# Softmax readings summed by a GpSimd DMA, one query buffer, a power root, and a new plan

## The chip, the core and the metric

The kernel runs on one core of one Trainium2 chip. The metric is the device time in microseconds of one execution; lower is better. The core's engines run side by side and meet at semaphores: PE (matmul), ACT (activation functions), DVE (vector work), POOL (GpSimd) and SP, which here only issues DMAs. SBUF is the on-chip memory, PSUM the eight banks into which PE writes.

## What is computed

Multi-query attention and a feed-forward block, both fed by the same layer norm, added to the input. Sequence S = 2048, width D = 640, 32 heads of 20 with one shared K and V, feed-forward width 1728, all in bf16:

```python
xn = _layernorm(x)
q = (xn @ wq).reshape(B, S, 32, 20).transpose(0, 2, 1, 3)
k = xn @ wk
v = xn @ wv
scores = einsum("bhqd,bkd->bhqk", q, k) * 20 ** -0.5
o = einsum("bhqk,bkd->bhqd", softmax(scores), v)
return x + o.transpose(0, 2, 1, 3).reshape(B, S, 640) @ wo + silu(xn @ w1) @ w2
```

## The kernel before

**Blocks.** The scores are cut into 2048 blocks of 128 keys by 512 queries for one head: 4 query chunks (`QC`), 8 groups of four heads per chunk, 16 key tiles. A step (`do_S`, matmuls at L1133) multiplies three or four blocks at once, each in a strip of 32 rows of PE, one PSUM bank per block. The value product PV (`do_pv`, L973) takes up to four items at once, one per head of the group, each in a strip of 32 columns.

**Two ways to the exponential.** Most blocks go to ACT: one activation (L1167) over one to three banks writes the exponentials into a ring `E` of 31 blocks, and each block is one PV item. The others go to DVE. The scores come out of PE scaled so that, clipped and converted to int16 (L1182, called p1), their bits read as bf16 are a coarse exponential. To make it finer, it is read three times: as it is (`Z`), and with 43 and with 86 added to the bits (`Y`, two planes). Each reading is multiplied by its own copy of V, weighted 1.0, 0.8047 and 0.625, in PSUM. So a DVE block is three PV items. Three DVE blocks make a set; `flush_z` issues a set's two additions, on POOL as 64-bit integer additions over the set (L1221, after a load of the library that holds them, `go_wide`; before that as 32-bit ones, L1227), or the first of them on DVE (L1215). `NZ` = 4 sets of buffers rotate.

**The rest of PE's work.** `mm4` (L872) does the query projections, the feed-forward block and the output projection, in jobs that fill in between steps. Tanh on ACT (L1379) with L1384 on DVE makes the SiLU. When a group of four heads is done, DVE copies its PSUM bank out (L1285), an SP transpose turns it (L1254), and L1269 and L1275 normalise it.

**The planner.** The program builds its own order. `Sched` holds one list per engine and modelled durations for each operation; it walks through modelled time, and at each moment picks the next instruction of each engine. What it chose is fixed in the program: the engines run in that order and wait on semaphores. `SEG` is a table of 64 rows, each for 32 score blocks, with the planner's thresholds: how much DVE backlog still lets a block go to DVE (`DVE_TH`, `DVE_TH2`), when PV may run, and so on. Its rows have a value that no name in `SEG_KEYS` takes, the last. An operation marked `lock` isn't planned on POOL and DVE at the same time; `late` is added to the modelled landing of a DMA.

**Queries.** `qT` holds the queries of two chunks, in two buffers. `qd_job` projects 128 columns for a chunk and DMAs copy its heads into their strips; two big copies (`qz`) fill the strips' constant rows first.

**The prologue.** Sixteen tiles of x are loaded, their mean and variance are taken on DVE (L1685, L1687) or, for the tiles in `ACT_STATS`, on ACT (L1670, L1673). The reciprocal root runs in batches of tiles (`BATCHES`) as two Newton steps, chains of some ten small instructions on POOL (`newton`, L1734 to L1758). The norm is applied on DVE (L1715) or POOL (L1711), the result is transposed by SP or PE. K and V follow; a second copy of K with an offset is made on POOL (L1838), the weighted copies of V on DVE (L1860).

Of the kernel before, what the change touches and what calls it, by code (L numbers as in the profile page):

```python
# [8 lines left out]
BF16 = mybir.dt.bfloat16  # L9
# [26 lines left out]
UT_LATE = 2.0  # L36
# [12 lines left out]
OFF_LO = 45.0  # L49
PH = ((0, 1.0), (43, 0.8046875), (86, 0.625))  # L50
# [5 lines left out]
NZ = 4  # L56
# [5 lines left out]
H0_STEP = 10  # L62
# [25 lines left out]
FOUR_FROM = 35  # L88
# [7 lines left out]
PV_HOLD = 12  # L96
# [3 lines left out]
DT = (5, 6, 7, 8, 9, 10, 11, 12, 14, 15)  # L100
NORM_P = 0.9
# [14 lines left out]
K1_ENG = "pool"  # L116
PV_MIN = 3
PV_GO = 9
PRO = "t0 t2 t1 p0 t3 k0 k1 p1 q1 v0 t4 k2 v1 k3 k4 t13 v2 k5 k6 v3 k7 d0"
ACT_STATS = (1, 4, 6, 12, 14, 15)  # L120
NW_ENG = ("pool", "pool", "pool")
NORM_ENG = ("pool", "dve", "dve", "dve", "pool", "dve", "dve", "dve", "dve", "pool", "dve", "pool")
# [5 lines left out]
            "ACT4", "SPLIT", "U2", "LOOK", "JOB_BANKS", "U_IDLE")  # L128
SEG = (
# [64 lines left out]
)  # L194
BATCHES = ((0, 4), (4, 10), (10, 16))
T_ACT = (0, 2, 6)


# [288 lines left out]
class Builder:  # L487
# [205 lines left out]
    def s_reads(self, bs, dvs=()):  # L693
        k = []
        for x in bs:
            g, kt, j = x
            c, h = g // 8, 4 * (g % 8) + j
            k += [("kT1" if x in dvs else "kT", kt // 2), ("kT", kt // 2), ("qb", c % 2, h)] + self.qkeys(c, h)
# [1242 lines left out]
```

## Time and profile before

| | us |
|---|---|
| median of 3 runs | 662.92 (662.53 to 663.67) |
| the profiled execution | 662.48 |
| its span, first to last instruction | 660.7 |
| clock of TensorE granted | 1.000 |
| the exponentials on ACT (L1167), 644 activations | 609.6 |
| p1 on DVE (L1182), 739 blocks | 476.4 |
| integer additions on POOL (L1221), 491 | 394.1 |
| PV matmuls (L973), 3526 | 266.7 |

The profile gives, for each engine, the time in which an instruction of it was running. PE's busy time overlaps with itself, since matmuls are pipelined and their ends are modelled. A line such as L1182 is the line of the program which recorded the operation. "Idle before" is the time in which an engine stood still ahead of a group's instructions, and the releaser is what ended most of it.

### The profile page before, as it was taken

To read this page: it belongs to the slowest core of one execution; us is meant where nothing else is said; L and a number is where in the kernel's file an instruction comes from. 1 tells how busy PE (TensorE), PEld (TensorE's weight loads), DVE (VectorE), ACT (ScalarE), POOL (GpSimd) and SP (SyncE) were. 2 spreads that over 40 slices of the span, in tenths; PEclk is the share of its full clock that TensorE was granted. 3 is DMA by queue.
4 is the path that set the end of the run, shared out by engine and by line. 5 is a ranking of instruction groups with operands and counts; after the bars stand their busy time and mean duration, and the time that the engine had idled before them with its cause. 6 is when DMAs were issued, how large, how long until landed. Compare 5 with 4: busy or idle time off the path is not lost.

```text
span 660.7 us, 22924 instructions
## 1 busy us (share of the span) xinstructions
PE 654.3 (99%) x9762; PEld 220.6 (33%) x9764; DVE 601.5 (91%) x1060; ACT 645.8 (98%) x735; POOL 420.3 (64%) x568
## 2 busy tenths in 40 slices
PE   8999999999999999999999999999999999999998
PEld 4432222323333333333333333333332333333334
DVE  7799999899999997999999979999999998999995
ACT  7899999999999999999999999999999999999995
POOL 6646667676776662676666744677666664766673
PEclk9999999999999999999999999999999999999999
DMA  7566300000004200001003210000000310011001
GB/s 212 97 237 195 88 18 11 10 13 13 14 20 72 73 10 10 10 10 18 18 11 57 63 39 10 18 10 8 12 19 10 77 55 25 10 18 34 11 10 42
DMA packets 52058, 27.89 MB, mean 42 GB/s; under 512 B 37910, under 2 KB 51318, under 8 KB 51958
## 3 DMA queue, kind: packets, MB, share of 16 engines
q1 hardware_dynamic: 50502, 26.22, 15.6%
q8 instruction: 78, 1.28, 0.8%
q10 hardware_dynamic: 1456, 0.22, 0.2%
q14 instruction: 22, 0.18, 0.1%
HBM read 11.44 MB, written 2.62 MB: 21 GB/s over the span
## 4 chain that ended last, share of the span: by engine, by line
PE 92%; ACT 3%; DVE 2%; DMA 2%; SPq 1%; issue 0%; DVEq 0%
PE psall L973 34%; PE psall L1133 29%; PE psall L872 27%; ACT sbt L1167 3%; DMA sbt<-sbt 1%; DVE sbt L1685 1%; DMA sbt<-in_A_x_dram 1%; SPq L1575 0%; DVE sbt L1715 0%; PE psall L1828 0%; PE psall L1369 0%; PE psall L1851 0%; ACT sbt L1379 0%; DVE sbt L1467 0%; DVE sbt L1820 0%
## 5 line engine op out<-in xcount | busy, mean ns | idle before, releaser
L1167 ACT ACTIVATE sbt<-psall 128x1024 bf16<-128x1024 f32 (+2 forms) x644 | 609.6, 1068 | 3.5 <-PE psall L1133 2.9
L1221 POOL INT64_ADD sbt<-sbt x491 | 394.1, 815 | 209.1 <-DVE sbt L1182 183.8
L1182 DVE TENSOR_SCALAR sbt<-psall 128x512 int16<-128x512 f32 x739 | 476.4, 684 | 37.1 <-PE psall L1133 27.6
L973 PE MATMUL psall<-sbt 128*32 128x512 bf16 x3526 | 266.7, 383 | 0.0
L1133 PE MATMUL psall<-sbt 32*128 32x512 bf16 x2048 | 243.6, 384 | 0.3 <-ACT sbt L1167 0.2
L872 PE MATMUL psall<-sbt 128*32 128x320 bf16 (+2 forms) x3939 | 218.3, 331 | 0.3 <-DVE sbt L1687 0.3
L1133 PEld LDWEIGHTS psall<-sbt 32*128 32x128 bf16 x2048 | 61.8, 91 | 235.2 <-issue 80.8
L872 PEld LDWEIGHTS psall<-sbt 128*32 128x32 bf16 x3939 | 85.6, 95 | 85.1 <-issue 50.2
L973 PEld LDWEIGHTS psall<-sbt 128*32 128x32 bf16 x3526 | 63.3, 95 | 99.5 <-issue 68.9
L1384 DVE SCALAR_TENSOR_TENSOR sbt<-sbt,psall 128x512 bf16<-128x512 bf16 x54 | 36.7, 682 | 6.5 <-ACT sbt L1379 6.0
L1379 ACT ACTIVATE sbt<-psall 128x512 bf16<-128x512 f32 x54 | 33.6, 629 | 0.4 <-PE psall L872 0.3
L1285 DVE CAST sbt<-psall 128x512 bf16<-128x512 f32 x32 | 21.9, 683 | 0.6 <-PE psall L973 0.4
L1275 DVE TENSOR_TENSOR sbt<-sbt 128x320 bf16<-128x320 bf16 x31 | 15.8, 510 | 0.0
L1448 DVE SCALAR_TENSOR_TENSOR sbt<-psall,sbt 128x320 bf16<-128x320 f32 x28 | 13.5, 484 | 1.6 <-PE psall L872 1.2
L848 PE MATMUL psall<-sbt 128*128 128x512 bf16 (+2 forms) x44 | 12.9, 447 | 1.4 <-DVE sbt L1624 1.2
L1467 DVE SCALAR_TENSOR_TENSOR sbt<-psall,sbt 128x320 bf16<-128x320 f32 x28 | 13.0, 482 | 1.2 <-PE psall L872 1.2
L1336 DVE TENSOR_SCALAR sbt<-psall 128x512 bf16<-128x512 f32 (+1 forms) x19 | 12.9, 678 | 0.1
L1685 DVE BATCH_NORM_STATS2 sbt<-sbt 128x6 f32<-128x320 bf16 x20 | 8.9, 471 | 3.4 <-DMA sbt<-in_A_x_dram 3.4
L1269 DVE RECIPROCAL sbt<-sbt 128x16 f32<-128x16 bf16 x31 | 7.6, 244 | 0.4 <-DMA sbt<-sbt 0.4
L848 PEld LDWEIGHTS psall<-sbt 128*128 128x128 bf16 x46 | 4.8, 112 | 7.5 <-issue 3.3
L1227 POOL TENSOR_TENSOR sbt<-sbt 128x768 int32<-128x768 int32 x4 | 5.9, 1465 | 0.5 <-DVE sbt L1182 0.5
L1464 ACT ACTIVATE sbt<-psall 128x320 bf16<-128x320 f32 x4 | 1.6, 437 | 4.4 <-PE psall L872 4.3
(72 smaller groups left out, 90.8 us busy)
## 6 DMA issues: line engine op xcount, KB each, us to landing
sbt<-in_A_x_dram SPq DMA_DIRECT2D x32, 160.0 KB, 3.7
out_dram<-sbt SPq DMA_DIRECT2D x15, 160.0 KB, 2.0
sbt<-in_B_w_dram SPq DMA_DIRECT2D x5, 432.0 KB, 5.3
sbt<-sbt SPq DMA_DIRECT2D x105, 20.0 KB
sbt<-in_B_w_dram SPq DMA_DIRECT2D x13, 160.0 KB, 3.0
sbt<-sbt SPq DMA_DIRECT2D x1, 1024.0 KB, 6.3
sbt<-sbt SPq DMA_TRANSPOSE x57, 2.5
sbt<-in_A_wo_dram SPq DMA_DIRECT2D x5, 160.0 KB, 3.0
```

The source lines that it names most:

```text
L848: return pe.matmul(self.bk(b, 0, n), self.zero[:, 0:P], self.zero[:, 0:n], start=True, stop=True)
L872: ins = pe.matmul(self.bk(b, 0, n, r, r + SLOT), w[:, r:r + SLOT], x, start=start, stop=stop, tile_position=(0, r), skip_group_check=True)
L973: ins = pe.matmul(self.bk(ub[k], 0, QW, r, r + SLOT), self.v[:, it.w, it.kt, :], it.x(), start=f, stop=False, tile_position=(0, r), skip_g ...
L1133: ins = pe.matmul(self.bk(bank[x]), self.kT[r:r + SLOT, kk, kt * P:(kt + 1) * P], self.qT[r:r + SLOT, g % 8, (g // 8) % 2, :], start=True, ...
L1167: return a.activation(self.E[:, b0 * QW:(b0 + na) * QW].rearrange("p (b n) -> p b n", n=QW), src, AF.Exp, scale=ACT_SCALE)
L1182: return v.tensor_scalar(self.Z[:, zs, zp * QW:(zp + 1) * QW], self.bk(bb), 0.0, ZMAX, ALU.max, ALU.min)
L1221: sc.new("pool", tp, lambda v, k=k, c=c: v.int64_add(self.Y[:, zs, k, 0:w].bitcast(I64), self.Z[:, zs, 0:w].bitcast(I64), c), zk + [("lib" ...
L1275: op = sc.new(eng, 0.067 + 16 * DH / 960.0, lambda v: v.tensor_tensor(dst, ut[:, :, :, 0:DH], rb, ALU.mult), [key, ("rL", up)], [("o", h0 ...
L1285: sc.new("dve", t_dve_ps(QW), lambda v: v.tensor_copy(self.U[:, up, :], self.bk(ub)), [("B", ub)], [("U", up)], prio=U_PRIO, name=f"Uev{g}")
L1379: sc.new("act", t_act(QW), lambda a: a.activation(t, src, AF.Tanh, scale=0.5), [("B", b)], [("tb", tp)], prio=TH_PRIO, name=f"th{c}_{fk}") ...
L1384: sc.new("dve", t_dve_ps(QW), lambda v: v.scalar_tensor_tensor(out=self.hT[0:rows, fk, :], in0=t, scalar=1.0, in1=src, op0=ALU.add, op1=AL ...
L1685: np_("dve", 0.41, lambda v, hf=hf: v.bn_stats(self.st6[:, n, hf, :], x[:, hf * 320:hf * 320 + 320]), self.xkeys(n), [("st6", n, hf)], pri ...
```

## The change

**Summed readings.** The offsets are 0, 41 and 87 now, and the first two readings carry the same weight, so V is kept in two copies: one for the readings 0 and 41, one for 87. Where `both` holds in `flush_z`, a DMA issued by POOL adds the set's `Z` to its first `Y` plane (384 KB, bf16), and each block becomes two PV items; elsewhere it stays three. `both` needs a full set, the loaded library, and a modelled POOL backlog (with the two additions, 1.6 us) under the new threshold `CB_TH`, the last value of the `SEG` rows. Of the 64 rows, 39 have it above 1.6 and 26 above 4; the 39 are rows 4, 6, 8, 10, 12, 14, 15, 16, 18, 19, 20, 23, 24, 26, 28, 30, 32 to 40, 42, 44, 46, 48, 50 to 54, 56, 58 and 60 to 62, counted from 0; most of the others have -9. The DMA is booked with 1.2 us on POOL and a landing of some 3.4 us more.

**Buffers.** `qT` holds one chunk instead of two; the second constant fill goes. `NZ` becomes 5.

**Prologue.** The Newton chains become an addition and a power on POOL, in six batches instead of three. The norm on POOL adds the negative mean and then multiplies. The second copy of K is made on DVE, so the library of 64-bit additions is loaded as soon as POOL's prologue work is done. ACT's table load goes ahead of the loads of wk and wv. Five tiles instead of six have their statistics on ACT, six instead of four their norm on POOL.

**Order.** Every row of `SEG` is new, and so are the order of the first jobs (`PRO`), some modelled times and thresholds, and with them the whole order of instructions.

```diff
-UT_LATE = 2.0
+UT_LATE = 3.0
-PH = ((0, 1.0), (43, 0.8046875), (86, 0.625))
+PH = (0, 41, 87)
+PW = (1.0, 0.77734375)
-NZ = 4
+NZ = 5
+POW_FIX = 0.45
+POW_COL = 0.145
+CB_COST = 1.2
+CB_LATE = 1.4
+CB_PRIO = 3.0
+CB_BYTES = 1050000
+CB_TH = -9.0
-K1_ENG = "pool"
+K1_ENG = "dve"
-ACT_STATS = (1, 4, 6, 12, 14, 15)
+ACT_STATS = (2, 4, 6, 12, 15)
-BATCHES = ((0, 4), (4, 10), (10, 16))
-T_ACT = (0, 2, 6)
+BATCHES = ((0, 2), (2, 4), (4, 8), (8, 9), (9, 11), (11, 16))
+T_ACT = (2, 4, 5, 6)
...
-        self.v = sb([P, 3, KT, SLOT], BF16)
-        self.qT = sb([P, HT, 2, QW], BF16)
+        self.v = sb([P, 2, KT, SLOT], BF16)
+        self.qT = sb([P, HT, QW], BF16)
...
@@ do_S
-            self.item(g, j, kt, 0, lambda zs=zs, zp=zp: self.Z[:, zs, zp * QW:(zp + 1) * QW].bitcast(BF16),
-                      [("Z", zs, zp)])
@@ flush_z
+        both = n == ZB and self.wide and back["pool"] + 2 * tp - sc.t["pe"] < CB_TH
+        if both:
+            y0 = self.Y[:, zs, 0, 0:w].bitcast(BF16)
+            z0 = self.Z[:, zs, 0:w].bitcast(BF16)
+            yk = [("Y", zs, 0, i) for i in range(n)]
+            op = sc.new("pool", CB_COST, lambda q: q.dma_start(out=y0, in_=z0, accum_op=ALU.add), zk + yk, yk,
+                        prio=CB_PRIO, name="cb")
+            op.dma = op.lock = True
+            op.sem = self.s_cb[zs]
+            op.mode = CB_BYTES
+            op.late = CB_LATE
+            self.cb_cnt[zs] += 1
+            op.inc_no = self.cb_cnt[zs]
         for i, (t, g, kt, j) in enumerate(self.zblocks):
+            if not both:
+                self.item(g, j, kt, 0, lambda i=i: self.Z[:, zs, i * QW:(i + 1) * QW].bitcast(BF16), [("Z", zs, i)])
             for k in range(2):
-                self.item(g, j, kt, k + 1, lambda k=k, i=i: self.Y[:, zs, k, i * QW:(i + 1) * QW].bitcast(BF16),
+                self.item(g, j, kt, k, lambda k=k, i=i: self.Y[:, zs, k, i * QW:(i + 1) * QW].bitcast(BF16),
                           [("Y", zs, k, i)])
@@ qd_job
         def consume(b):
+            assert c == 0 or self.bp >= GB * (8 * (c - 1) + (hi - 1) // DH // 4 + 1)
@@ prologue
+        def root(a, b_, pr):
+            ve = self.tmp[:, 0, a:b_]
+            h = self.half[:, :]
+            hb = bass.AP(self.half, h.offset, [list(h.ap[0]), [0, b_ - a]])
+            add = np_("pool", 0.2, lambda g: g.tensor_scalar(ve, self.mv[:, a:b_, 1], EPS, None, ALU.add), mvk(a, b_),
+                      [("va", a)], prio=pr, name="eps")
+            add.then = np_("pool", POW_FIX + POW_COL * (b_ - a), lambda g: g.tensor_tensor(self.rstd[:, a:b_], ve, hb, ALU.pow),
+                           [("va", a), ("half",)], [("rs", a)], prio=pr, name="root")
...
```

In `do_S` the block's first PV item, issued there before, is left out; `flush_z` issues it with the others, so without `both` it can run only once the whole set is flushed.

More of the change, by code (lines that the diff above doesn't have):

```diff
@@ L549, in alloc @@
         self.eps = sb([P, 1], F32)
+        self.half = sb([P, 1], F32)
+        self.nm = sb([P, NT], F32)
         self.cy = sb([P, 2], I32)
@@ L697, in s_reads @@
             c, h = g // 8, 4 * (g % 8) + j
-            k += [("kT1" if x in dvs else "kT", kt // 2), ("kT", kt // 2), ("qb", c % 2, h)] + self.qkeys(c, h)
+            k += [("kT1" if x in dvs else "kT", kt // 2), ("kT", kt // 2), ("qb", 0, h)] + self.qkeys(c, h)
         return k
@@ L1351, in consume @@
                 op.inc_no = len(ops)
-        reads = [("xnT", 4 * c + i) for i in range(4)] + [("wqd", 0), ("wqd", 1), ("qz", c % 2)]
+        reads = [("xnT", 4 * c + i) for i in range(4)] + [("wqd", 0), ("wqd", 1), ("qz", 0)]
         if c >= 2:
@@ L1567, in prologue @@
         self.ut_cnt = [0, 0]
+        self.s_cb = [sem(f"cb{i}") for i in range(NZ)]
+        self.cb_cnt = [0] * NZ
         self.s_oT = [sem(f"oT{i}") for i in range(4)]
@@ L1576, in load_x @@
                         self.xkeys(n)[:2] if n < NT - 1 else self.xkeys(n)[:1], P * D * 2, sem=s_x[n])
-            op.late = 0.1 if n == 0 else 0.3 if n == 1 else 1.2 if n < 13 else 2.2
+            op.late = (0.1, 0.2, 0.4, 0.6)[n] if n < 4 else 1.4 if n < 13 else 2.2
             op.inc_no = 1
@@ L1587, in load_w @@
             sc.note(op, (), [tag])
+        sc.new("pool", 0.1, lambda g: g.memset(self.eps[:, :], EPS), [], [("eps",)], name="pool")
+        sc.new("act", 1.4, lambda ac: ac.activation(self.tmp[:, 1, 0:1], self.eps[:, :], AF.Exp), [("eps",)],
+               [("warm",)], prio=0.0, name="table")
         for src, k, j in ((self.A_wk, "k", 0), (self.A_wv, "v", 1)):
             sv = src.rearrange("(c p) d -> p c d", p=P)
-            load_w("act", k, [lambda q, sv=sv, j=j: q.dma_start(self.kv_st[:, j, :, :], sv)], ("st", k), 25600)
+            load_w("act", k, [lambda q, sv=sv, j=j: q.dma_start(self.kv_st[:, j, :, :], sv)], ("st", k), 25600, (),
+                   [("warm",)], 1.5 + j)
         for n in range(4):
@@ L1647, in prologue @@
         pool(0.9, lambda g: g.memset(self.v[:, :, :, :], 0.0), [], [("v0",)] + [("v", i) for i in range(8)])
-        for k in range(3):
-            pool(0.15, lambda g, k=k: g.memset(self.v[:, k, :, DH:DH + 1], 0.5 * PH[k][1]), [("v0",)],
+        for k in range(2):
+            pool(0.15, lambda g, k=k: g.memset(self.v[:, k, :, DH:DH + 1], 0.5 * PW[k]), [("v0",)],
                  [("v0",)] + [("v", i) for i in range(8)])
@@ L1760, in prologue @@
-        np_("act", 1.4, lambda ac: ac.activation(self.tmp[:, 1, 0:1], self.eps[:, :], AF.Exp), [("eps",)],
-            [("warm",)], prio=0.0, name="table")
+            if eng == "pool":
+                np_("pool", 0.87, lambda v: v.tensor_scalar(
+                    xa(n), self.xslot(n), self.nm[:, n:n + 1], self.rstd[:, n:n + 1], ALU.add, ALU.mult),
+                    self.xkeys(n) + [("nm", ra), ("rs", ra)], [("xn", n)], prio=prio, name=f"norm{n}").lock = True
+                return
+            np_("dve", 0.36, lambda v: v.tensor_scalar(
+                xa(n), self.xslot(n), self.mv[:, n, 0:1], self.rstd[:, n:n + 1], ALU.subtract, ALU.mult),
+                self.xkeys(n) + [("mv", n), ("rs", ra)], [("xn", n)], prio=prio, name=f"norm{n}").lock = True
@@ new lines, in root @@
+        def root(a, b_, pr):
[6 more added lines that the diff above has]
+                           [("va", a), ("half",)], [("rs", a)], prio=pr, name="root")
+            add.lock = add.then.lock = True
+            if any(NORM_ENG[n - 4] == "pool" for n in range(max(a, 4), b_)):
+                np_("pool", 0.22, lambda g: g.tensor_scalar(self.nm[:, a:b_], self.mv[:, a:b_, 0], -1.0, None, ALU.mult),
+                    mvk(a, b_), [("nm", a)], prio=pr + 0.01, name="nm").lock = True
@@ L1766, in prologue @@
                 self.batch[n] = a
-            newton(a, b_, 0.001 * i if b_ <= 4 else 0.3, NW_ENG[i])
+            root(a, b_, 0.001 * i if b_ <= 4 else 0.3)
             if b_ <= 4:
@@ L1858, in consume @@
                 sv = self.bk(b, 0, 20 * m).rearrange("p (i d) -> p i d", d=DH)
-                for k in range(3):
+                for k in range(2):
                     sc.new("dve", 0.07 + m * DH / 960.0, lambda v, k=k: v.tensor_scalar(
-                        self.v[:, k, n0:n1, 0:DH], sv, PH[k][1], None, ALU.mult),
+                        self.v[:, k, n0:n1, 0:DH], sv, PW[k], None, ALU.mult),
                         [("B", b), ("v0",)], [(kk, i) for i in range(n0 // 2, n1 // 2) for kk in ("v", "vv")], prio=0.6,
```

117 lines of the change are left out of this document (32 added, 85 removed), and 128 rows, old and new, of the table SEG.

## The prediction

> **What bounds the kernel now.** I read the engines' busy time first, then the same by stage, then the groups of instructions, the waits, and the score evictions stretch by stretch. The engine row shows three engines that could each be the limit:
>
> ```profile
> PE 654.3 (99%) x9762; PEld 220.6 (33%) x9764; DVE 601.5 (91%) x1060; ACT 645.8 (98%) x735; POOL 420.3 (64%) x568
> ```
>
> PE's 99% is modelled, with pipelined matmuls overlapping, so it proves little. The table by stage says where the others have room (columns: the stretch in us, its length, busy us and count of PE, PEld, DVE, ACT, POOL, clock, DMA share, GB/s):
>
> ```profile
> 0.00:32.00 32.00, 29.24 (x287) 13.87 (x289) 24.32 (x80) 26.44 (x47) 20.42 (x70) 1.00 0.63 157
> 32.00:64.00 32.00, 31.70 (x423) 9.79 (x420) 30.94 (x56) 31.97 (x37) 17.99 (x23) 1.00 0.64 209
> 64.00:640.00 576.00, 575.75 (x8742) 188.54 (x8738) 533.13 (x901) 573.87 (x636) 374.40 (x466) 1.00 0.12 27
> 640.00:661.00 21.00, 17.59 (x320) 8.35 (x317) 13.12 (x26) 13.51 (x18) 7.45 (x11) 1.00 0.09 33
> ```
>
> From 64 to 640 us ACT idles 576.00 - 573.87 = 2.1 us: there it sets the pace. DVE has 576 - 533.13 = 42.9 us left in that stretch, POOL 202 us. In the first 32 us ACT idles 5.6 us, in the tail 660.7 - 640 - 13.51 = 7.2 us. The clock is 1.00 throughout. Hence the stretch from 64 to 640 shortens only as ACT gets less work. The groups (busy us, mean ns; then idle before) give the exchange rate:
>
> ```profile
> L1167 ACT ACTIVATE sbt<-psall 128x1024 bf16<-128x1024 f32 x577 | 544.5, 1054 | 2.9 <-PE psall L1133 2.5
> L1182 DVE TENSOR_SCALAR sbt<-psall 128x512 int16<-128x512 f32 x739 | 476.4, 684 | 37.1 <-PE psall L1133 27.6 <-PE psall L973 0.5 <-POOL sbt L1221 0.3
> L1221 POOL INT64_ADD sbt<-sbt x491 | 394.1, 815 | 209.1 <-DVE sbt L1182 183.8 <-DVE sbt L1275 21.0 <-PE psall L1133 2.3
> L973 PE MATMUL psall<-sbt 128*32 128x512 bf16 x3526 | 266.7, 383 | 0.0
> ...
> L1167 ACT ACTIVATE sbt<-psall 128x1536 bf16<-128x1536 f32 x44 | 65.1, 1484 | 0.5 <-PE psall L1133 0.4
> ```
>
> A score block exponentiated on ACT costs (1484 - 1054) = 0.43 us there, the difference between a three-block and a two-block activation. On DVE (L1182) it costs 0.684 us. DVE has 739 of the 2048 blocks; the PV items bear that out, 1309 + 3 x 739 = 3526, for a DVE block is multiplied three times and an ACT block once. So PE pays for each block moved away from ACT. Three further views say whether PE is what keeps the planner from moving more. Waits (us in total, times, longest):
>
> ```profile
> PEld psall L1133 <- DVE sbt L1182: 69.7, 175, 0.4
> ...
> PEld psall L1133 <- ACT sbt L1167: 42.5, 106, 0.5
> ...
> PEld psall L973 <- POOL sbt L1221: 13.8, 61, 0.2
> ```
>
> PE waits 69.7 + 42.5 us for score banks to be read out, in pieces of at most 0.5 us, and DVE 27.6 us for scores (the L1182 row): nobody is far ahead. The score evictions of DVE by stretch (busy us and count):
>
> ```profile
> 64.00:128.00 64.00, 50.27 (x79) 1.00 0.15 39
> 128.00:192.00 64.00, 53.24 (x85) 1.00 0.06 15
> 192.00:256.00 64.00, 45.56 (x71) 1.00 0.21 45
> ...
> 384.00:448.00 64.00, 43.74 (x68) 1.00 0.05 11
> ...
> 512.00:576.00 64.00, 44.84 (x69) 1.00 0.18 43
> ```
>
> In 192-256, 384-448 and 512-576 DVE takes 71, 68 and 69 blocks; in the other six from 79 to 85 (the two shown are their ends), some 81. The same view of L872, the feed-forward and projection matmuls (busy us and count of PE, then PEld), shows why:
>
> ```profile
> 128.00:192.00 64.00, 18.67 (x376) 7.83 (x376) 1.00 0.06 15
> 192.00:256.00 64.00, 26.65 (x436) 9.54 (x440) 1.00 0.21 45
> ...
> 384.00:448.00 64.00, 27.74 (x476) 10.56 (x476) 1.00 0.05 11
> ```
>
> 27 to 28 us of such work in the poor stretches against 18.67 in a rich one: there PE's load, not DVE's, keeps blocks on ACT. That is the room which a cheaper DVE block could open.
>
> **Part 1: the summed readings.** Where the planner allows it, a set of three DVE blocks has its first two readings added by a DMA, so each block needs two PV items instead of three: three items, three quarters of a four-wide PV slot. Sixteen PV matmuls against eight give the slot:
>
> ```profile
> 309.21 1.05 PE L973 MATMUL psall<-sbt 128*32 128x512 bf16 x16
> ...
> 311.60 0.61 PE L973 MATMUL psall<-sbt 128*32 128x512 bf16 x8
> ```
>
> (1.05 - 0.61)/2 = 0.22 us, so a summed set saves PE 0.165 us. How many sets? There are 739/64/3 = 3.85 sets per row of the table of 64. A set is summed if POOL's backlog beyond PE, plus the 1.6 us that the code books for two adds, lies under the row's last number. That can hold in 39 rows (over 1.6); in 26 it is over 4. At most 39 x 3.85 = 150 sets, at least half of the 26 rows' sets, 50. I take 85% of the 26 rows' and half of the other 13's, 85 + 25 = 110. Of the rows that I put in the three poor stretches (18-23, 37-43, 50-56, at about 9.9 us a row) some 15 of 20 are on, against some 24 of 44 elsewhere: the sums go where the trace shows PE short. PE saves 110 x 0.165 = 18.2 us.
>
> This is worth nothing unless blocks move. Each moved block gives ACT 0.43 us, costs PE at most 2 items, 0.11 us, and DVE 0.684 us. If the span falls by 0.43n, PE must shed 0.43n too: 18.2 >= 0.54n, n <= 33; DVE: 42.9 >= (0.684 + 0.43)n, n <= 39. Filling half of the gap of about 12 blocks in the three stretches gives 18; with a few elsewhere I take n = 20: **-8.6 us**. Bounds: 0 (nothing moves), and with 150 sets DVE's 39 blocks, -17. With 50 sets PE allows 15, -6.5.
>
> What it adds: 110 POOL instructions that issue a DMA. No row shows a DMA issued by POOL. The longest issue near it is SP's transpose:
>
> ```profile
> 304.34 1.20 SPq L1254 DMA_TRANSPOSE sbt<-sbt  x1
> ```
>
> I take 1.2 us of POOL, between nothing and about a library load (last rival): 132 us against 202 us free, so POOL stays under the end, at (420 + 132)/655 = 84%. Behind a waiting issue stand the next adds. A set then costs POOL 2 x 0.815 + 1.2 = 2.83 us against one set every 660.7/247 = 2.7 us, so full sums in a row build a backlog, which is what the threshold cuts. Landing has bounds from copies of 160 and 768 KB against the sum's 384 KB:
>
> ```profile
> out_dram<-sbt SPq DMA_DIRECT2D x15, 160.0 KB, 2.0
> ...
> sbt<-sbt SPq DMA_DIRECT2D x1, 768.0 KB, 4.4
> ```
>
> 2.0 to 4.4 us, plus the issue: I take 4.5 us in all, 3.2 of it landing. The fifth set of buffers gives back 2.7 us of that; before, DVE waits for PV matmuls only 0.5 us in the whole run (the L1182 row, releaser L973), so reuse of the buffers is not close to binding. In all sets the first reading now becomes a PV item with the set instead of at once, up to 2.7 us later; the other two readings, waiting at the same place, hide that. What can be late is the summed PV item: PE's order is fixed, and a sum that lands later than planned stops PE. The nearest row is PE's wait for POOL's adds, 13.8 us in 61 waits, 0.23 us each. I take that for one set in eight: **+3 us**; bounds 0 and 110 x 0.23 = +25.
>
> GpSimd's port was another doubt. The adds of POOL, min/median/max in ns:
>
> ```profile
> L1221 POOL INT64_ADD sbt<-sbt x491: 395/824/830, 47.3 to 649.9; - x164
> ```
>
> They never stretch (max 830 against median 824) although L1182 fills 72% of the span (476.4 of 660.7 us) and so runs beside most of them, so L1182 doesn't block POOL. [...]
>
> **Part 2: the prologue.** The reciprocal root of the first four tiles runs on POOL as a chain of ten:
>
> ```profile
> 7.70 0.19 DVE L1687 BATCH_NORM_AGGREGATE sbt<-sbt 128x2 f32<-128x12 f32 x1
> ...
> 7.97 0.26 POOL L1734 TENSOR_SCALAR sbt<-sbt 128x4 f32<-128x4 f32 x1 [0.93 <-DVE sbt L1687]
> ...
> 10.55 0.20 POOL L1750 TENSOR_TENSOR sbt<-sbt 128x4 f32<-128x4 f32 x1
> ...
> 11.00 1.46 DVE L1715 TENSOR_SCALAR sbt<-sbt 128x640 bf16<-128x640 bf16 x4
> ...
> 18.19 4.13 ACT L1167 ACTIVATE sbt<-psall 128x1536 bf16<-128x1536 f32 x3 [0.21 <-PE psall L1133]
> ```
>
> From the aggregate's end (7.89) to the first norm (11.00) are 3.1 us. After: an add (0.26, the L1734 row) and one power, no row: between 0.2 (the small POOL rows) and 1.5; I take 0.7, as the code books, so about 2 us are saved, and tiles 0 and 1 go in a batch of their own. The first exponential at 18.19 hangs on weights and transposes too. One tile's statistics leave ACT:
>
> ```profile
> L1673 ACT ACTIVATE sbt<-sbt 128x640 bf16<-128x640 bf16 x6 | 4.4, 734 | 0.1
> L1670 ACT ACTIVATE sbt<-sbt 128x640 bf16<-128x640 bf16 x6 | 4.4, 730 | 1.2 <-DMA sbt<-in_A_x_dram 1.1
> ```
>
> with two read-outs of 0.19, 1.85 us less ACT work. The loads of wk and wv now stand behind ACT's first table load; that is hidden as long as they land before the norms (11.00 above), after which k's matmuls come. On DVE:
>
> ```profile
> L1715 DVE TENSOR_SCALAR sbt<-sbt 128x640 bf16<-128x640 bf16 x12 | 4.9, 451 | 0.0
> ...
> L1860 DVE TENSOR_SCALAR sbt<-psall 128x80 bf16<-128x80 f32 x12 | 2.8, 233 | 1.4 <-PE psall L1851 1.4
> L1215 DVE TENSOR_SCALAR sbt<-sbt 128x1536 int16<-128x1536 int16 x5 | 2.7, 550 | 0.0
> ...
> L1673 ACT ACTIVATION_READ_ACCUMULATOR sbt<-sbt 128x1 f32 x6 | 1.1, 191 | 0.0
> ```
>
> eight k copies come from POOL (0.2 to 0.55 each, +2 us), four V copies go (-0.9), two norms go to POOL (-0.9, and +1.7 on POOL), a statistic comes (+1). DVE idles 7.7 us in those 32, so this is level. The integer library is loaded once POOL's norms are done instead of after the last k copy. Removing the second query buffer drops one DMA; a query job now writes after the previous chunk's group is done, 54 steps before use, so no wait is expected. Of the 2 us of chain and the 1.85 us of ACT I count half, since the one opens the other's idle time anyway: prologue **-2 us**, bounds +1.5 (the k copies at their longest, nothing else gained) and -4. The tail is unchanged.
>
> **Sum** against the profiled execution's 662.48 us: -8.6 + 3 - 2 = -7.6, 654.9. The median of the runs is 0.44 us above that execution: I predict **655 us**. This case by itself: 648 to 660.
>
> **Rivals.** (a) *The sums come late*: the landing, added to the port wait or to competing transfers, is missed by PE on most sets. From 10.6/110 = 0.10 us per set it eats the gain; at 0.165 us (18 us) the time is 662.9 + 18 - 10.6 = 670. For it: POOL's adds already make PE wait 61 times, and PE has no idle time to absorb it. Against: the wait is short each time, and the fifth set. (b) *ACT stays full*: PE's relief goes into filler and waits, no block moves; only the prologue counts: 661. For it: ACT is the first bound and DVE has already 93%. Against: the three poor stretches. The same time comes if the backlog test is seldom met and hardly a set is summed. (c) *All of DVE's room is used*: -17 - 2 + 1 gives 645. For it: POOL and PE would allow it at 150 sets. Against: DVE's 27.6 us of waits for scores don't vanish. (d) *Library reloads*: the two loads cost
>
> ```profile
> POOL sbt L1242 <- issue: 8.5, 1, 8.5
> ...
> POOL sbt L1247 <- issue: 6.7, 1, 6.7
> ```
>
> and if issuing a DMA threw the integer code out, each sum would cost 15 us of POOL and the time would double or more. No row says that a DMA needs a load; this gets 0.02 and stands outside the range.
>
> **Chances.** Forecast 0.53, (a) 0.23, (b) 0.12, (c) 0.10, (d) 0.02. The kernel's measurement tells 0.2% (1.3 us) from no change. Of (b), 0.06 is faster by more than that, 0.05 the same, 0.01 slower; of (a) 0.22 is slower and 0.01 faster. Faster 0.70, same 0.05, slower 0.25. The range from 645 to 671 leaves out the far ends of (a), half of (c) and (d), some 0.17.
>
> **What would show it.** L1182's count in the profile after: about 760 (739 or less means (b); near 780, (c)). PV matmuls: 3526 + 40 - 330 = about 3240. POOL at 80 to 88%; about 110 DMAs issued by it. ACT still without idle between 64 and 640 us, DVE above 94%, and the poor stretches with 74 or more blocks each. First exponential at about 17 us. Rival (a) would show as PE waiting on the summing DMA, 0.1 us or more a set, and as ACT idling on scores. The prediction is wrong if ACT's busy time doesn't fall by 5 us or if it falls and ACT idles instead.

## The result and the profile after

The changed kernel takes 665.0 us (median of 20 runs, 661.1 to 668.9) against 662.93 (20 runs): 1.0032 times, 95% interval 1.0018 to 1.0046. It is a little slower; 655 was forecast. The profiled execution took 664.61 us, its span is 662.8 and its mean clock 0.997.

The engine row:

```profile
PE 644.8 (97%) x9470; PEld 214.5 (32%) x9472; DVE 612.0 (92%) x1088; ACT 636.8 (96%) x720; POOL 522.8 (79%) x667
```

ACT has 9.0 us less to do than before (645.8), so the planned relief is there. The table by stage (the columns as before) says what became of it:

```profile
64.00:640.00 576.00, 566.29 (x8428) 181.99 (x8421) 542.52 (x925) 564.31 (x629) 479.12 (x588) 1.00 0.53 100
```

Between 64 and 640 us ACT is idle for 576.00 - 564.31 = 11.7 us, against 2.1 before: 9.6 us of new idle time have eaten 9.0 us of relief. PE stands still 9.7 us, before 0.25. The last two columns name a suspect: the DMA engines are busy 0.53 of the time in place of 0.12.

The groups, with different shapes apart, then the sums with their issue times and landing:

```profile
L1176 ACT ACTIVATE sbt<-psall 128x1024 bf16<-128x1024 f32 x609 | 574.1, 1053 | 12.9 <-PE psall L1142 11.5
L1191 DVE TENSOR_SCALAR sbt<-psall 128x512 int16<-128x512 f32 x762 | 489.0, 683 | 34.3 <-PE psall L1142 26.6 <-POOL sbt L1228 0.2
L1228 POOL INT64_ADD sbt<-sbt x506 | 436.2, 942 | 102.7 <-DVE sbt L1191 71.2 <-DVE sbt L1297 18.3 <-DVE sbt L1222 5.0
L982 PE MATMUL psall<-sbt 128*32 128x512 bf16 x3233 | 249.5, 384 | 6.8 <-DMA sbt<-sbt 5.9 <-POOL sbt L1228 0.9
...
L1176 ACT ACTIVATE sbt<-psall 128x1536 bf16<-128x1536 f32 x22 | 31.7, 1480 | 0.0
```

```profile
L1242 POOL DMA_DIRECT2D sbt<-sbt x113: 850/874/1333, 66.5 to 640.5; - x113
...
DMA to landing us min/median/max: 3.8/4.6/7.9
```

The plan did what was forecast: 762 blocks on DVE, 3233 PV matmuls, 113 sums. New are ACT's 11.5 us of waits for scores (2.5 and 0.4 before) and PE's waits for a DMA. The waits (us, times, longest; a wait of PV for a DMA counts twice where it holds both the weight load, PEld, and the matmul, PE):

```profile
ACT sbt L1176 <- PE psall L1142: 11.5, 17, 1.8
PEld psall L982 <- DMA sbt<-sbt: 8.0, 11, 1.9
...
PE psall L982 <- DMA sbt<-sbt: 5.9, 8, 1.6
...
PE psall L881 <- DMA sbt<-sbt: 2.3, 1, 2.3
```

So few of the 113 sums are waited for, and one wait (L881) is not for a sum but for a transpose. Two places of the timeline show how such waits come about (start, length, engine, line; the length of an SP row is that of the issue and the landing is listed apart: 2.70 us in the row of L1276 below, and 5.1 to its landing). The first, with the landing of the four transposes of L1421:

```profile
199.99 0.86 POOL L1242 DMA_DIRECT2D sbt<-sbt  x1
200.14 2.70 SPq L1276 DMA_TRANSPOSE sbt<-sbt  x1
202.89 6.89 SPq L1421 DMA_TRANSPOSE sbt<-sbt  x4
202.94 0.87 POOL L1242 DMA_DIRECT2D sbt<-sbt  x1 [1.22 <-DVE sbt L1297]
205.91 1.20 POOL L1242 DMA_DIRECT2D sbt<-sbt  x1
208.05 0.59 PE L881 MATMUL psall<-sbt 128*32 128x320 bf16 x12 [2.34 <-DMA sbt<-sbt]
```

```profile
DMA to landing us min/median/max: 4.1/5.7/7.1
```

Three sums in six microseconds meet five transposes, that of the chunk's last group (L1276) and the four that bring the chunk's output to the output projection (L1421); PE waits 2.34 us for these. What follows is in the stretches (us, PE busy and count, granted clock, DMA share, GB/s; the share adds up the times of all transfers under way and exceeds 1 here, up to 1.67):

```profile
206.00:208.00 2.00, 0.00 (x0) 1.00 1.11 206
208.00:210.00 2.00, 1.95 (x35) 0.89 1.13 187
210.00:212.00 2.00, 2.00 (x19) 0.50 1.67 139
212.00:214.00 2.00, 2.00 (x22) 0.76 0.48 92
```

The clock falls to half for (0.11 + 0.50 + 0.24) x 2 / 0.5 = 3.4 us after the wait has ended. The second place:

```profile
380.20 1.38 SPq L1494 DMA_DIRECT2D out_dram<-sbt  x1
381.02 0.88 POOL L1242 DMA_DIRECT2D sbt<-sbt  x1
381.62 0.44 SPq L1539 DMA_DIRECT2D sbt<-in_A_x_dram  x1
...
383.61 0.86 POOL L1242 DMA_DIRECT2D sbt<-sbt  x1
383.97 0.53 SPq L1494 DMA_DIRECT2D out_dram<-sbt  x1
384.54 1.53 SPq L1539 DMA_DIRECT2D sbt<-in_A_x_dram  x1
388.27 0.12 PEld L982 LDWEIGHTS psall<-sbt 128*32 128x32 bf16 x8 [1.92 <-DMA sbt<-sbt]
```

Here two sums meet stores of the output (L1494) and loads of x for the residual (L1539), and it is a sum that lands late: these two take 7.2 and 7.9 us against the median of 4.6.

### The profile page after: what moved, and what is told of

Same layout as the page of the kernel before. It is cut to its first block, busy times and chain, and to the rows that moved or that the text cites. A ratio compares the mean times of both kernels' runs of the same rounds, so it can differ in the third digit from the quotient of the medians.

```text
span 662.8 us, 22461 instructions
## 1 busy us (share of the span) xinstructions
PE 644.8 (97%) x9470; PEld 214.5 (32%) x9472; DVE 612.0 (92%) x1088; ACT 636.8 (96%) x720; POOL 522.8 (79%) x667
## 4 chain that ended last, share of the span: by engine, by line
PE 81%; DVE 8%; DMA 8%; POOL 2%; issue 0%; ACT 0%; SPq 0%; DVEq 0%
PE psall L982 29%; PE psall L1142 26%; PE psall L881 23%; DMA sbt<-sbt 7%; DVE sbt L1191 5%; POOL sbt L1228 2%; DVE sbt L1490 1%; DVE sbt L1407 1%; PE psall L1820 1%; DVE sbt L1307 1%; PE psall L857 1%; DMA sbt<-in_A_x_dram 1%; PE psall L1392 0%; DVE sbt L1714 0%; DVE sbt L1740 0%
## 5 line engine op out<-in xcount | busy, mean ns | idle before, releaser
L1176 ACT ACTIVATE sbt<-psall 128x1024 bf16<-128x1024 f32 (+2 forms) x633 | 603.0, 1067 | 12.9 <-PE psall L1142 11.5
L1191 DVE TENSOR_SCALAR sbt<-psall 128x512 int16<-128x512 f32 x762 | 489.0, 683 | 34.3 <-PE psall L1142 26.6
L1228 POOL INT64_ADD sbt<-sbt x506 | 436.2, 942 | 102.7 <-DVE sbt L1191 71.2
L982 PE MATMUL psall<-sbt 128*32 128x512 bf16 x3233 | 249.5, 384 | 6.8 <-DMA sbt<-sbt 5.9
L1142 PE MATMUL psall<-sbt 32*128 32x512 bf16 x2048 | 247.6, 385 | 0.8 <-DVE sbt L1828 0.3
L881 PE MATMUL psall<-sbt 128*32 128x320 bf16 (+2 forms) x3939 | 223.0, 332 | 2.6 <-DMA sbt<-sbt 2.3
L1242 POOL DMA_DIRECT2D sbt<-sbt x113 | 114.8, 1016 | 9.8 <-DVE sbt L1297 7.7
L881 PEld LDWEIGHTS psall<-sbt 128*32 128x32 bf16 x3939 | 83.5, 95 | 87.7 <-issue 57.8
L982 PEld LDWEIGHTS psall<-sbt 128*32 128x32 bf16 x3233 | 58.7, 94 | 103.5 <-issue 72.2
L857 PE MATMUL psall<-sbt 128*128 128x512 bf16 (+3 forms) x41 | 11.7, 429 | 1.3 <-DVE sbt L1653 1.2
L1820 PE MATMUL psall<-sbt 128*128 128x256 bf16 x40 | 6.1, 274 | 1.2 <-DMA sbt<-sbt 1.2
```

The costliest lines, as they stand in the source:

```text
L857: return pe.matmul(self.bk(b, 0, n), self.zero[:, 0:P], self.zero[:, 0:n], start=True, stop=True)
L881: ins = pe.matmul(self.bk(b, 0, n, r, r + SLOT), w[:, r:r + SLOT], x, start=start, stop=stop, tile_position=(0, r), skip_group_check=True)
L982: ins = pe.matmul(self.bk(ub[k], 0, QW, r, r + SLOT), self.v[:, it.w, it.kt, :], it.x(), start=f, stop=False, tile_position=(0, r), skip_g ...
L1142: ins = pe.matmul(self.bk(bank[x]), self.kT[r:r + SLOT, kk, kt * P:(kt + 1) * P], self.qT[r:r + SLOT, g % 8, :], start=True, stop=True, ti ...
L1176: return a.activation(self.E[:, b0 * QW:(b0 + na) * QW].rearrange("p (b n) -> p b n", n=QW), src, AF.Exp, scale=ACT_SCALE)
L1191: return v.tensor_scalar(self.Z[:, zs, zp * QW:(zp + 1) * QW], self.bk(bb), 0.0, ZMAX, ALU.max, ALU.min)
```

## The experiments

All runs keep the changed kernel's order of instructions. Sums are counted from 0 in order of issue; where times name a sum, they are its issue in the profile after.

**Again.** The changed kernel unaltered, beside the next three.

> The changed kernel once more, for its time beside the others on this chip: 0 to 1% above the kernel before, with its runs spread over several us; in its profile PE waits for DMAs 8 to 20 us in all between 64 and 640 us and ACT idles 8 to 14 us there.

Measured: 663.96 us (12 runs, 662.2 to 669.3), ratio 1.0026 (1.0005 to 1.0047). This is the mark for the others.

**The bytes out of all sums.**

```diff
             z0 = self.Z[:, zs, 0:w].bitcast(BF16)
+            y0, z0 = y0[:, 0:16], z0[:, 0:16]
```

> Every summing DMA moves 16 of the 1536 columns of its set; the rest of the sums is left out. Order, waits and POOL's instructions stay. Theory D (the sums' bytes on the DMA engines make sums and transposes land late, and PE's fixed order stops for them): landing falls to 2 to 3 us, PE's waits for DMAs between 64 and 640 us fall below 1 us, ACT idles at most 3 us there, and the time is 651 to 654 us. Rival O (the new order as such is no better, stalls come from elsewhere): 660 us or more. Rival P (issuing from POOL slows its additions and these are late): the mean of the additions stays above 900 ns, PE waits for POOL grow, and the time stays above 658.

Measured: 653.14 us (5 runs within 0.5 us), ratio 0.9847 (0.9830 to 0.9863). The stage and, from the list of DMA issues, the sums (KB each, median us to landing):

```profile
64.00:640.00 576.00, 575.51 (x8592) 186.34 (x8586) 551.32 (x942) 573.37 (x640) 486.88 (x597) 1.00 0.17 25
```

```profile
sbt<-sbt POOLq DMA_DIRECT2D x113, 4.0 KB, 2.3
```

With the same instructions in the same order, PE and ACT are full again and the time is 9.9 us under the kernel before. The bytes of the sums cost 663.96 - 653.14 = 10.8 us. The issues on POOL, still 113, and the additions, as long as in the profile after (437.0 us), can cost little between 64 and 640 us, where PE stands still 0.5 us and ACT 2.6; that the program's end is 1.1 us longer than before, here too, is taken up below.

**Which sums.** The first version cuts the three sums of the first place above (26, 27, 28). The second cuts fourteen, those issued within some 9 us ahead of one of PE's larger waits in the profile after. The third, a control, cuts fourteen others that lie apart from these.

```diff
+            if sum(self.cb_cnt) in (26, 27, 28):
+                y0, z0 = y0[:, 0:16], z0[:, 0:16]
```

> Only the three summing DMAs around 200 to 206 us move 16 columns, the rest as in the changed kernel; the rest of these three sums is left out. Theory D, part one (they delay the four transposes of the attention output of chunk 0, PE stands 2.3 us and then runs a while at half clock): the 2.34 us wait goes, no half clock near 210 us, and the time falls by 3 to 5 us against the changed kernel on this chip. If only late sums count and not the transposes: less than 1.5 us.

> The fourteen summing DMAs that land around PE's visible waits move 16 columns, the other 99 are whole; the rest of these fourteen sums is left out. Theory D with few places that matter: 653 to 657 us, most of what the kernel with all sums cut gains. If lateness is spread over all sums: 658 or more, at most half of that gain.

> Fourteen other summing DMAs, spread over the run and more than 6 us from those cut before, move 16 columns; the rest of these fourteen sums is left out. Theory D (few places, where several transfers meet): no more than 1.5 us faster than the changed kernel, 662 to 664.5 us. If any fourteen sums fewer relieve PE alike: 654 to 658.

Measured: three sums 660.89 us (659.1 to 664.9), ratio 0.9974 (0.9956 to 0.9991); fourteen 654.24 (653.8 to 654.3), ratio 0.9862 (0.9846 to 0.9879); the control 665.57 (661.2 to 669.3), ratio 1.0020 (0.9995 to 1.0046). Fourteen sums carry 663.96 - 654.24 = 9.7 of the 10.8 us, 0.7 us each; the other 99 carry 1.1 us, 0.01 each; fourteen arbitrary ones carry nothing measurable (the control's interval is 1.7 us to either side). With the three sums cut, the wait at 208 us is gone and the clock stays at 1.00 there. In the version with fourteen cut, the four transposes at the first place land sooner:

```profile
DMA to landing us min/median/max: 2.4/2.5/2.8
```

The median is 2.5 us against 5.7 with the sums whole, and PE doesn't wait for them. So bytes that POOL's DMAs move delayed transposes that SP had issued.

**What the sums meet.** Cut are the bytes of the residual loads and output stores together, then of the loads alone and the stores alone.

```diff
-q.dma_start(self.xres[:, i, :], self.xv[:, n, :])
+q.dma_start(self.xres[:, i, 0:16], self.xv[:, n, 0:16])
-q.dma_start(self.outv[:, n, :], ost)
+q.dma_start(self.outv[:, n, 0:16], ost[:, 0:16])
```

> All sums whole; the loads of x for the residual and the stores of the output move 16 of 640 columns, the rest of both is left out. Theory D1 (the sums are late where SP's loads and stores share the DMA engines with them): the sums issued at 381 and 384 us land within 6 us instead of 7 to 8, PE's waits for DMAs fall by 3 us or more, the time falls by 3 us or more against the changed kernel. Rival D2 (the sums delay each other, issued every 2.2 to 2.6 us while each takes over 4): waits and time within 1.5 us of the changed kernel's.

> The kernel after, in its own order, with every sum whole and every output store whole; only the sixteen loads of the residual x tiles move 16 of 640 columns (the residual is left out of most of the output). With loads and stores both cut the time was 659.4 us, 4.6 under the unchanged kernel of the batch before. If the loads are what the sums meet (four of them stand in the profile beside the stalls at 388 us and 545 us), this gives about 660 and those two stalls go; if the stores are, 663 to 664 and the stalls stay. The stall near 208 us, ended by a transpose of a group's output, has no load beside it and should stay either way, as should the half clock behind it in the runs that have it.

> The kernel after, in its own order, with every sum and every residual load whole; only the sixteen output stores move 16 of 640 columns (most of the output is left unwritten). If the loads are what the sums meet, about 663 us, of which some 1 us is the tail, where the last stores land later than before; if the stores are, about 660 and the stalls at 388 us and 545 us are gone. The two cuts together gave 4.6 us: a sum of the two gains near that would mean that each stall has one cause, a larger one for either alone that loads and stores bring the same stalls together.

Measured: both 659.39 us (657.2 to 664.3), ratio 0.9945 (0.9916 to 0.9975); loads alone 664.6 (659.8 to 667.0), ratio 1.0010 (0.9989 to 1.0031); stores alone 1.0009 (0.9981 to 1.0037), from 659.2 us up. With both cut, PE's matmuls wait 2.6 us for sums in place of 5.9, and the two sums of the second place (58 and 59) land after 4.2 and 5.5 us in place of 7.2 and 7.9, as D1 had it. The two single cuts seem to do nothing, against both theories. Their profiles, one execution of ten each, show what can hide a gain. Stores cut, the waits, then the landing of the four transposes at the first place and PE's wait for them:

```profile
PE psall L881 <- DMA sbt<-sbt: 7.0, 1, 7.0
PEld psall L982 <- DMA sbt<-sbt: 5.7, 14, 0.8
PE psall L982 <- DMA sbt<-sbt: 3.4, 7, 1.5
```

```profile
DMA to landing us min/median/max: 8.5/9.0/9.6
```

```profile
212.81 0.99 PE L881 MATMUL psall<-sbt 128*32 128x320 bf16 x12 [6.97 <-DMA sbt<-sbt]
```

The waits on sums fell, 5.7 from 8.0 and 3.4 from 5.9 us, and sums 58 and 59 land after 5.1 and 6.1 us (5.2 and 6.1 with the loads cut). But in this execution the four transposes took 8.5 to 9.6 us to land, PE waited 6.97 us for them, and it ran at half clock until 218.3 us. The same wait is 6.76 us in the profile with the loads cut, 2.34 in the profile after, 0.80 in that of the repeated kernel, 3.85 in the control's and 0.88 with loads and stores both cut: it differs from run to run, and can hide what the cuts give back. So this wait was taken out and the question put again:

> The kernel after, in its own order; of the fourteen sums cut before, eleven move 16 of 1536 columns (their readings keep the second alone), and the three issued between 200 and 206 us are whole. If these three, with the transposes that they meet, are one stall of 0.8 to 7 us with up to 3.4 us of half clock behind it, the time is 654.2 (fourteen cut) plus that: 656 to 663 with nearly the whole spread of the kernel after, the profile's only long wait at 208 us. If the spread comes from chance elsewhere, the runs lie within 1 us of each other near 656.

> The kernel after, in its own order; the three sums between 200 and 206 us and the sixteen residual loads move 16 columns each (their readings keep the second alone, and most of the residual is left out). With the three sums alone cut it was 660.9. If the loads are what the other sums meet, 657 to 658; if the stores are, 660 to 661. If either is enough to make the sums late, both this and its sister stay near 660.5.

> The kernel after, in its own order; the three sums between 200 and 206 us and the sixteen output stores move 16 columns each (their readings keep the second alone, and most of the output is left unwritten). If the loads are what the other sums meet, 660, the tail alone gaining up to 1 us; if the stores are, 657 to 658. If either is enough to make the sums late, near 660.5.

Measured: eleven cut, the three whole, 659.76 us (4 runs, 657.7 to 660.4), ratio 0.9943 (0.9922 to 0.9965); three sums and the loads 657.25 (4 runs), 0.9927 (0.9899 to 0.9955); three sums and the stores 657.97 (4 runs), 0.9923 (0.9903 to 0.9942). By the first, the place at 200 to 206 us alone costs about (0.9943 - 0.9862) x 663 = 5.4 us (cut before the others it gave back 3.1), and spreads its few runs over 2.7 us where fourteen cut spread over 0.6. By the other two, with the three sums cut, taking out the loads gives about (0.9974 - 0.9927) x 663 = 3.1 us more and the stores 3.4, and the profiles agree: PE's matmuls wait 7.1 us for sums with the three cut alone, 3.3 with the loads cut too and 4.2 with the stores. Neither of the two is the culprit alone: taking either out makes room, an outcome that the expectations of this pair did not list.

**Versions that compute the whole.** For chosen sets the sum is not made, and a third reading is multiplied instead: `Z` as an additional matmul in the planned slot, so that the order stays. A copy of 4 KB to a scratch buffer keeps the semaphores.

```diff
+            raw = sum(self.cb_cnt) in (27, 32, 35, 58, 92)
+            if raw:
+                y0, z0 = self.scr[:, zs, :], z0[:, 0:16]
...
+                if both and raw and k == 0:
+                    self.item(g, j, kt, k, lambda y=y, i=i: (self.Z[:, zs, i * QW:(i + 1) * QW].bitcast(BF16), y()),
+                              [("Y", zs, k, i), ("Z", zs, i)])
```

> The same for all fourteen sets: the waits go as in the kernel with fourteen sums cut (654.2), and the extra matmuls cost 0 to 14 x 3 x 0.22 = 9.2 us: 656 to 661 us, about 658 if half of the extra matmuls share a slot with another.

> Seven of the sums around PE's waits are not made: their blocks have three readings again, the third as one more matmul in the planned PV slot; the order of everything else stays, and a DMA of 16 columns stands in the place of each sum. Theory D: PE loses at most 7 x 3 x 0.22 = 4.6 us and gains most of 9 us: 656 to 660 us, faster than both kernels. If the extra matmuls cost their full price and half the waits stay: 661 to 664.

> The whole computation. Three sets (issued in the profile at 202.94, 381.02 and 538.92 us, one in each of the three clusters that stall PE most) are not summed: their blocks are read three times, nine matmuls more in all, at about 0.2 us each (the price that the version with fourteen such sets showed), so 1.8 us more of PE. By the theory that the cost sits where three sums in a row meet the transposes and loads, taking out the middle one gives back most of the three stalls (2.3 + 1.1 us and the half clock behind the first, 1.6 + 0.6 us, 1.1 us), 5 to 7 us, and the time is 659 to 661, under the seven-set version (662.2) and under the kernel before (662.9). By the rival, that the delay is spread over all sums and only shows where PE has least slack, the stalls move to the next sum and the time is 663 to 665.

> As the version with three sets, with two more (228.99 and 263.02 us), which come before the stalls at 235 to 238 us (0.9 us) and 269 us (1.07 us). Fifteen more matmuls, about 3 us of PE, against stalls of up to 7 to 9 us: 659 to 661 by the theory of clusters, no better than the three-set version, since the two sets added cost 1.2 us and give back at most 2. By the rival of a spread delay 663 to 665.

> The whole computation; as the five-set version (660.5), and the set whose sum was issued at 205.91 us is read three times too. Three matmuls more, 0.6 us. The five-set version's profile still waits 0.98 us for the transpose near 207 us, its four transposes taking 5.98 us. If that is the last of this cluster, this gives 659.5 to 661, no better; its spread should be smaller than 5.5 us (658.7 to 664.2). By the rival, that every set left unsummed shifts the later sums against the transposes at random, it may land anywhere from 659 to 664, as the three- and seven-set versions did.

Measured: fourteen sets 662.8 us, ratio 0.9993 (0.9977 to 1.0009); seven 662.2, 0.9980 (0.9958 to 1.0001); three 663.96, 1.0000 (0.9986 to 1.0015); five 660.47 (658.7 to 664.2), 0.9950 (0.9932 to 0.9967); six 661.51, 0.9978 (0.9963 to 0.9993). Seven lies in the second range of its forecast, fourteen above its own. Fourteen has the same large DMAs as the version with fourteen sums cut and takes 662.8 - 654.24 = 8.6 us more. The extra matmuls are less than half of that. Three of them, beside eight that were planned, lengthen the stretch by 0.84 - 0.62 = 0.22 us together, the price of one four-wide slot (the version with fourteen cut, then this one):

```profile
382.77 0.62 PE L982 MATMUL psall<-sbt 128*32 128x512 bf16 x8
```

```profile
388.58 0.84 PE L985 MATMUL psall<-sbt 128*32 128x512 bf16 x11
```

The 42 sit in 18 places of PE's order, and the delay that arises at these adds up to 4.0 us, some 0.1 us a matmul and not the 0.2 that the expectations of the later versions carry on. Laid beside each other, the two profiles show two more parts: 2.2 us arise between 26 and 33 us, ahead of every extra matmul, where PE waits 2.07 us for a DMA (1.26 with fourteen cut) and the clock is half for 3.4 us afterwards, and 1.1 us behind PE's last matmul. The rest is in small waits.

Three came out in the rival's range, but not by the rival's way: in its profile the three stalls are shorter or gone (0.85 us at 208 us for 2.34, 0.27 at 390 for 1.62, none near 545). Against them stand about 1 us for nine matmuls, an end that is 2.2 us longer (it comes 6.4 us behind PE's last matmul, 5.9 to 6.3 in the other four versions, 4.2 in the profile after), and the places that it doesn't touch; its largest waits left there, by the timeline:

```profile
235.01 0.61 PE L985 MATMUL psall<-sbt 128*32 128x512 bf16 x8 [1.15 <-DMA sbt<-sbt]
268.09 0.61 PE L985 MATMUL psall<-sbt 128*32 128x512 bf16 x8 [0.85 <-DMA sbt<-sbt]
```

Five takes these two as well, and its stage is full:

```profile
64.00:640.00 576.00, 574.17 (x8558) 185.38 (x8551) 550.56 (x940) 571.59 (x637) 484.15 (x596) 1.00 0.54 98
```

PE stands still 1.8 us there, with the DMA engines as busy as in the changed kernel (0.54 and 0.53). It is faster than the kernel before by 0.3 to 0.7%, and by the ratios to it faster than the changed kernel (1.0032) too, whose span it beats by 5.9 us in the profiled executions; its own is the fastest of its eleven runs. The sixth set, expected to change little, brought no more; its profile waits 2.08 us for the transposes again, though two of the three sums there are gone; what delays them then wasn't settled. How much of the difference between five, six and seven is real stays open: their runs overlap (659.9 to 666.2 for seven, 659.4 to 664.3 for six), though the intervals of five and six touch only at 0.9963 to 0.9967.

## Why the prediction was wrong

**Right: the trade.** 760 DVE blocks were forecast and 762 came, 3240 PV matmuls and 3233, 110 sums and 113, 80 to 88% of POOL and 79%. Without the sums' cost the forecast stood at 662.48 - 10.6 = 651.9 us; with their bytes out the kernel takes 653.1. The size per block was somewhat off: the exponentials on ACT fell by 609.6 - 603.0 = 6.6 us for 23 blocks, 0.29 each and not 0.43; with the bytes out they take 601.3 us, 0.36 each. What keeps it under 0.43 wasn't worked out. The rest of ACT's 9.0 us is the prologue and the smaller work, which was costed apart.

**Right: the prologue.** The power takes what the code books, and the first exponential starts 1.58 us earlier (18.19 before):

```profile
6.21 0.74 POOL L1750 TENSOR_TENSOR sbt<-sbt 128x2 f32<-128x2 f32 x1
...
16.61 3.71 ACT L1176 ACTIVATE sbt<-psall 128x1536 bf16<-128x1536 f32 x3
```

**Partly right: where the blocks move.** The poor stretches were to take 18 of 20 moved blocks and 74 or more each; score evictions by stretch, busy us and count:

```profile
192.00:256.00 64.00, 47.21 (x74) 0.97 0.48 94
...
384.00:448.00 64.00, 45.85 (x71) 1.00 0.66 124
...
512.00:576.00 64.00, 45.03 (x70) 1.00 0.70 136
```

74, 71 and 70, against 71, 68 and 69: seven of the 23 moved there, the others into the rich stretches. PE's stalls lie in these three stretches, though; with the bytes out they hold 81, 75 and 73.

**Wrong: "I take that for one set in eight: +3 us".** This term measured 10.8 us. Its row was PE's wait for POOL's adds, 0.23 us at a time, and those adds, 815 ns each, never took more than 830. The sums delayed SP's transposes, and SP's loads and stores delayed the sums: with fourteen sums cut four transposes land after 2.5 us and not 5.7, and with loads and stores cut two sums land after 4.2 and 5.5 us and not 7.2 and 7.9. The DMA share of SP's transfers stood in the table by stage of before, 0.12, while the change was to add 113 x 384 KB. Nothing in the sum of the forecast priced this meeting. The number of waits was guessed about right (one set in eight is 14; PE's weight loads waited 11 times), their size was not: 0.7 us for each of fourteen sums, since single waits reach 1.9 and 2.3 us in the rows above, not 0.23, and the longest comes through a transpose that the forecast did not have as a thing that could become late. The prediction named the sign of it: wrong if ACT's busy time "falls and ACT idles instead", and so it came.

**Wrong too, but small: "The tail is unchanged."** From PE's last matmul to the end of the span it was 3.1 us before, and it is 4.2 now. What ends last is POOL's closing instruction, `DRAIN` (duration in ns, start in us; before, then after):

```profile
L1880 POOLq DRAIN  x1: 6917/6917/6917, 650.3 to 650.3; - x1
```

```profile
L1872 POOLq DRAIN  x1: 13945/13945/13945, 648.6 to 648.6; - x1
```

Before, it is over at 657.3 us and SP's, at 660.5, ends the program; now it is over at 662.6, and SP's at 661.4. It ends 0.8 to 1.9 us behind SP's in the profiles of the changed kernel and its versions with bytes cut, with 4 KB in every sum too (1.0), and 2.3 to 3.4 us behind in the five versions that compute the whole without some of them. No run shows what POOL waits for there. With this, 7.8 + 1.1 of the 10 us between the forecast and the measured time are named.

**The landing** was taken as 4.5 us with its issue and had a median of 4.6: right. But the bound, 4.4 us of landing and 1.2 of issue, was no bound: the longest took 7.9. PE's fixed order paid for the longest, with waits of up to 1.9 us, not for the median.

**Rival (a)** had this outcome: waits on the summing DMA, ACT idle on scores, and 0.10 us per set as the point from which the gain is gone. The mean came out at 10.8/113 = 0.096. Its picture, "missed by PE on most sets", does not hold: 99 sums cost 1.1 us together. Of the 10.8 us, between 3.1 and 5.4 belong to the three sums at 200 to 206 us with the transposes, the wait and the half clock behind it, and the rest of the 9.7, 4.3 to 6.6, to the other eleven, which meet loads, stores or each other. How much of it the sums cost one another wasn't tried.

**GpSimd's port.** The issues took 850 to 1333 ns, median 874, and but for the program's end no run shows a cost of theirs: with 4 KB a sum they are as long (851 to 1333 ns, median 874), and PE and ACT are full (575.51 and 573.37 of 576 us). No run leaves the issues out, and none shows the port wait that rival (a) adds to the landing; the transfers that compete, its other way, are what the runs showed.

## What to carry to other kernels

Moving work to the DMA engines was not free here: 99 sums cost 1.1 us together, but the other fourteen, with other transfers beside them, 9.7. So lay the new transfers beside those that are there on a timeline, those of other queues too, and ask which small transfer with a fixed taker (here a transpose) will land late, before costing the mean. In this order fixed ahead, the cost of 113 transfers sat in the few places where they crowd; cutting the bytes of one group at a time, with a control group of the same size, finds them. A single wait that differs from run to run (0.80 to 6.97 us here) can hide what an experiment gives back, so take it out and ask again. And before the difference of two times is put down to one cause, lay the two orders beside each other and see where it arises.

## What the runs showed of the hardware

**Half clock after short idle.** In the repeated kernel PE waits once for 1.62 us, and the granted clock then falls. The wait, and two stretches of 3.41 us (us, busy us and count of PE, PEld, DVE, ACT, POOL, clock, DMA share, GB/s):

```profile
386.89 0.61 PE L982 MATMUL psall<-sbt 128*32 128x512 bf16 x8 [1.62 <-DMA sbt<-sbt]
```

```profile
384.49:387.90 3.41, 1.79 (x31) 0.44 (x23) 2.14 (x6) 1.88 (x3) 2.04 (x3) 1.00 1.08 278
387.90:391.31 3.41, 3.41 (x31) 0.49 (x23) 1.85 (x3) 2.51 (x3) 1.63 (x2) 0.50 0.11 33
```

The profile after had a wait of the same 1.62 us at 388 us and kept its clock there. Two stretches of that profile, the one ahead of its half clock and the one with most of this wait, show what differed:

```profile
206.14:209.55 3.41, 1.50 (x31) 0.81 (x35) 0.85 (x3) 1.62 (x3) 0.97 (x2) 1.00 1.07 199
387.04:390.45 3.41, 2.18 (x30) 0.55 (x30) 1.97 (x4) 1.88 (x3) 1.72 (x3) 1.00 0.77 190
```

The clock changed in steps of 3.413 us: from its fall at 209.55 us in the profile after to its last one, behind the program's end at 663.52, are 133.0 of them. The half clock lasted 3.4 us there, 6.8 with eleven sums cut and 10.2 with the stores cut: one, two and three steps. Counted so, PE stood still 3.41 - 1.79 = 1.62 us of one step in the repeated kernel and 1.91 in the profile after, but the wait at 388 us was divided, and 1.23 us of it lay in one step. In the eight places between 64 and 640 us where the clock falls in these profiles, PE stood still 1.6 to 3.1 us of the step before; where it stood still up to 1.5 us in a step at full clock, the clock stayed. So a wait of the same 1.62 us cost half of a step more, by estimate 3.41/2 = 1.7 us, or nothing, as it lay on the steps. The shortest stop ahead of a fall, 1.6 us, is about half a step.

**Additions beside issues.** Before, no integer addition took longer than 830 ns by its record; now the records reach 1606 and their mean is 942 against 815 (945 with 4 KB a sum). POOL isn't slower for that, as one place shows (start, length):

```profile
164.34 1.20 POOL L1242 DMA_DIRECT2D sbt<-sbt  x1
164.97 2.24 POOL L1228 INT64_ADD sbt<-sbt  x2
166.71 1.33 POOL L1242 DMA_DIRECT2D sbt<-sbt  x1
```

An issue and two additions, 1.20 + 2.24 = 3.44 us by their records, take 166.71 - 164.34 = 2.37 us from one issue to the next, since the records overlap. Two additions at the old 0.815 us leave 0.74 us for the issue.
